# Decode attention over two caches on one core: who releases the value slot, when the denominators are gathered, and a projection on four column strips

## The chip, the cores and the metric

One core of one Trainium2 chip; the other cores are idle. The metric is the device time of one execution in microseconds (us), as the median of several executions. Ratios are computed as the mean time of one kernel's fast runs over that of the other's fast runs of the same rounds, so they are not quite the ratios of the medians quoted beside them. Where a sentence speaks of a "span", it is the profiled execution. In this kernel TensorE (PE in the profiles, PEld its weight loads) multiplies matrices into PSUM tiles, whose names begin with ps; DVE and ScalarE (ACT) copy and compute between PSUM and SBUF tiles; SP (its queue is SPq) issues the loads from device memory into SBUF.

## The reference, cut to what matters

Two attention blocks with one query token each, outputs concatenated. A has 32 heads with 32768 keys each; B has 32 query heads over 8 key heads, and only the last 4096 keys count.

```python
# A: q = x@wq; k, v: [32 heads, 32768 keys, 128]; out = softmax(q k^T / sqrt(128)) v, then @ wo
# B: the same with 8 key heads, each shared by 4 query heads, and a window of 4096 keys
o = einsum("bhqk,bhkd->bhqd", softmax(scores), v)
return concatenate([a, b], axis=-1)          # bf16, [1, 1, 1024]
```

So A alone reads 32 heads x (8 MiB of keys + 8 MiB of values), 537 MB of the 570 MB in all, and uses each byte once.

## The kernel before

Each head of A passes through these steps. SP issues all large loads in one queue, in the order K(0), V(0), K(1), V(1), ...; keys have three thirds of a buffer (a head uses two), values one slot of 8 MiB.

1. TensorE transposes the keys (8 per PSUM bank), DVE copies them to SBUF, TensorE makes scores on four column strips (psS).
2. DVE finds the maximum, ScalarE the exponentials (with the row sums in an extra column of `oc`), TensorE transposes them (psPT).
3. TensorE multiplies with the values, 64 matmuls on four strips, into psACC ("the products").
4. DVE sums four blocks of psACC into `oc` ("the sums"), and two small f32 matmuls gather `oc` into row g of psG: column 128 ("the denominators") and columns 0 to 127.

After the loop come the division, the spreading of A's and B's results to 128 partitions and the two projections with `wo`.

```python
    def emit_PV(self, name, g):
        ...                                  # 64 matmuls, c = 0..3 are column strips
        pv = self.op("pe", mm, self.landed("v", 0 if name == "A" else g), self.ptread, self.accread, to="dve")
        for i in (0, 1) if name == "A" else (g,):
            self.free["v"][i] = pv           # the next value load waits for this
        oc = t["oc"][g % 2][:, 0:DH]
        for j in range(4):                   # four sums on DVE, waiting for pv
            ...
        self.accread = o

    def emit_gather(self, name, g):
        ...
        for c, c2, to in ((DH, DH + 1, None), (0, DH, "dve")):
            self.gath = self.op("pe", lambda e, c=c, c2=c2: e.matmul(
                self.G[0:32, c0 + c:c0 + c2], lhsT=win, rhs=t["oc"][g % 2][:, c:c2], start=False, stop=True,
                skip_group_check=True), self.accread, self.sread, dep, to=to)
```

One thing in the helper matters. An operation raises one semaphore only, that of one waiting engine (`to`). If a second engine waits for it, the next operation of the same engine whose `to` is free carries that signal. Here the products signal DVE, and so the release of the value slot to SP is carried by the first gather matmul, which stands behind the four sums.

```python
    def emit_proj(self, name, bank, off):    # called for B, then for A
        for part in range(len(cuts) - 1):    # A's wo comes in 4 parts, B's in 2
            def mm(e, part=part):
                for a in range(cuts[part], cuts[part + 1]):     # 32 matmuls of 128x1 by 128x512
                    inst = e.matmul(bank[0:1, 0:512], lhsT=t["oz"][:, a:a + 1], rhs=wo[:, 512 * a:512 * a + 512],
                                    start=(a == 0), stop=(a == 31), skip_group_check=True)
            ...
```

## Time and profile before

| | |
|---|---|
| median of the first 3 runs | 1338.86 us (1338.84 to 1342.12) |
| median of 11 runs, three later sessions | 1342.8, 1342.33, 1341.78 us |
| span of the profiled run | 1340.9 us |
| last packet of the weights lands | 1332.25 us |

The page's head, its DMA row (busy tenths of the 16 DMA engines in 40 slices of the span) and the chain of waits by engine, kernel before:

```profile
span 1340.9 us, 28815 instructions
...
DMA  9999999999999999999999999999999999999996
...
DMA 68%; PE 28%; DVE 3%; issue 0%; ACT 0%; SPq 0%
```

Who the DMA queue's own sequencer (SPq) waited for; the first line is the value loads, the second mostly the key loads:

```profile
engine line waited for: us in total, times, longest us
SPq L283 <- PE psG L599: 743.7, 32, 23.9
SPq L283 <- PE psS L507: 524.9, 35, 27.8
```

And one head in the timeline (start, length, engine, line, what; in brackets the idle time before and what ended it):

```profile
894.27 6.10 PE L573 MATMUL psACC<-vbuf,ptsb 128*4 128x512 bf16 x64 [0.69 <-ACT ptsb L548]
...
900.43 0.35 DVE L585 TENSOR_SCALAR oc_A<-psACC,hot_A 128x128 f32<-128x128 f32 x1 [8.32 <-PE psACC L573]
900.81 1.12 DVE L587 SCALAR_TENSOR_TENSOR oc_A<-psACC,hot_A,oc_A 128x128 f32<-128x128 f32 x3
...
902.08 0.44 PE L599 MATMUL psG<-oc_A,hw 128*32 128x1 f32 x4 [1.72 <-DVE oc_A L587]
902.31 0.33 SPq L283 DMA_DIRECT2D vbuf<-in_A_v_cache_dram  x1
...
904.96 5.92 PE L485 MATMUL psT<-ident,kbuf 128*128 128x128 bf16 x64 [2.44 <-DMA kbuf<-in_A_k_cache_dram]
```

The products end at 900.37. The value load goes out 1.94 us later, at 902.31. The keys issued before it land at 904.92, so there were still 2.61 us of keys in flight. I call this distance the lead of the value issue.

The end of the kernel, the two projections and the last copy:

```profile
1323.32 8.36 PE L629 MATMUL psS<-kbuf,oz_B 128*1 128x512 bf16 x32
...
1331.52 7.07 PE L629 MATMUL psPT<-kbuf,oz_A 128*1 128x512 bf16 x32
...
1338.63 0.68 DVE L633 CAST out_sb<-psPT 1x512 bf16<-1x512 f32 x1 [6.23 <-PE psPT L629]
```

### The profile page before, as it was taken

To read this page: it belongs to the slowest core of one execution; us is meant where nothing else is said; L and a number is where in the kernel's file an instruction comes from. 1 tells how busy PE (TensorE), PEld (TensorE's weight loads), DVE (VectorE), ACT (ScalarE), POOL (GpSimd) and SP (SyncE) were. 2 spreads that over 40 slices of the span, in tenths; PEclk is the share of its full clock that TensorE was granted. 3 is DMA by queue.
4 is the path that set the end of the run, shared out by engine and by line. 5 is a ranking of instruction groups with operands and counts; after the bars stand their busy time and mean duration, and the time that the engine had idled before them with its cause. 6 is when DMAs were issued, how large, how long until landed. Compare 5 with 4: busy or idle time off the path is not lost.

```text
span 1340.9 us, 28815 instructions
## 1 busy us (share of the span) xinstructions
PE 960.0 (72%) x13272; PEld 667.2 (50%) x13272; DVE 804.6 (60%) x1660; ACT 54.8 (4%) x167; POOL 2.0 (0%) x15
## 2 busy tenths in 40 slices
PE   3756668776676877666786867678777667777777
PEld 3544446554444555444455544445555444555552
DVE  3655556765556676555676655566765555667572
ACT  0000000000000000000000000000000000000000
POOL 0000000000000000000000000000000000000000
PEclk9777788888778898787888878888887878888888
DMA  9999999999999999999999999999999999999996
GB/s 395 442 427 428 422 426 438 432 420 428 436 409 438 438 409 438 438 434 432 416 436 434 411 438 426 420 438 438 432 428 422 438 438 438 438 432 420 427 439 284
DMA packets 12932, 570.66 MB, mean 426 GB/s; under 512 B 1522, under 2 KB 1524, under 8 KB 1780
## 3 DMA queue, kind: packets, MB, share of 16 engines
q1 hardware_dynamic: 12628, 570.43, 99.0%
q8 instruction: 12, 0.20, 0.1%
q10 hardware_dynamic: 288, 0.00, 0.0%
q14 instruction: 4, 0.03, 0.0%
HBM read 570.43 MB, written 0.00 MB: 425 GB/s over the span
## 4 chain that ended last, share of the span: by engine, by line
DMA 68%; PE 28%; DVE 3%; issue 0%; ACT 0%; SPq 0%
DMA kbuf<-in_A_k_cache_dram 65%; PE psT L485 23%; PE psS L507 3%; DMA kbuf<-in_B_k_cache_dram 3%; DVE kt L488 3%; PE psACC L573 1%; PE psS L629 1%; PE psPT L629 1%; DVE oc_A L587 0%; ACT psb L535 0%; PE psPT L545 0%; DVE tr_in L524 0%; DVE b_A L530 0%; SPq L283 0%; DVE m L527 0%
## 5 line engine op out<-in xcount | busy, mean ns | idle before, releaser
L488 DVE COPY kt<-psT 128x1024 bf16<-128x1024 bf16 x1056 | 655.7, 684 | 210.2 <-PE psT L485 208.7
L485 PE MATMUL psT<-ident,kbuf 128*128 128x128 bf16 x8448 | 579.5, 234 | 137.5 <-DMA kbuf<-in_A_k_cache_dram 125.5
L485 PEld LDWEIGHTS psT<-ident,kbuf 128*128 128x128 bf16 x8448 | 540.1, 106 | 229.8 <-DMA kbuf<-in_A_k_cache_dram 133.6
L573 PE MATMUL psACC<-vbuf,ptsb 128*4 128x512 bf16 (+1 forms) x2112 | 189.2, 536 | 23.3 <-ACT ptsb L548 22.0
L507 PE MATMUL psS<-kt,qw 128*32 128x512 bf16 x2048 | 157.6, 385 | 15.5 <-DVE kt L488 15.5
L585 DVE TENSOR_SCALAR oc_A<-psACC,hot_A 128x128 f32<-128x128 f32 x32 | 11.2, 351 | 254.8 <-PE psACC L573 254.8
L573 PEld LDWEIGHTS psACC<-vbuf,ptsb 128*4 128x4 bf16 (+1 forms) x2112 | 61.0, 112 | 142.7 <-issue 95.6
L545 PE MATMUL psPT<-ident,psb 128*128 128x128 bf16 x136 | 20.2, 302 | 127.9 <-ACT psb L535 127.9
L545 PEld LDWEIGHTS psPT<-ident,psb 128*128 128x128 bf16 x136 | 11.5, 128 | 137.5 <-ACT psb L535 137.3
L535 ACT ACTIVATE psb<-psS,nb_A 128x512 bf16<-128x512 f32 x32 | 22.0, 687 | 1177.9 <-DVE nb_A L534 1177.9
L507 PEld LDWEIGHTS psS<-kt,qw 128*32 128x32 bf16 x2048 | 34.0, 95 | 58.0 <-DVE kt L488 31.4
L599 PE MATMUL psG<-oc_A,hw 128*32 128x128 f32 (+1 forms) x128 | 14.1, 220 | 54.9 <-DVE oc_A L587 54.9
L599 PEld LDWEIGHTS psG<-oc_A,hw 128*32 128x32 f32 x128 | 6.5, 109 | 70.1 <-issue 70.1
L587 DVE SCALAR_TENSOR_TENSOR oc_A<-psACC,hot_A,oc_A 128x128 f32<-128x128 f32 x96 | 33.7, 351 | 3.4
L524 DVE TENSOR_REDUCE tr_in<-psS 128x1 f32<-128x512 f32 x34 | 23.5, 692 | 17.5 <-PE psS L507 17.5
L527 DVE COPY m<-tr_a 1x16 f32<-1x16 f32 (+1 forms) x136 | 22.3, 164 | 2.6
L530 DVE COPY b_A<-mr_A 1x16 f32<-1x16 f32 x128 | 21.1, 165 | 2.4
L548 ACT ACTIVATE ptsb<-psPT 128x512 bf16<-128x512 bf16 x34 | 20.3, 597 | 30.5 <-PE psPT L545 30.5
L441 PE MATMUL psACC<-x_B,vbuf 128*128 128x1 bf16 x128 | 3.5, 165 | 13.2 <-DMA vbuf<-in_B_wq_dram 13.2
L441 PEld LDWEIGHTS psACC<-x_B,vbuf 128*128 128x128 bf16 x128 | 3.5, 104 | 13.1 <-issue 13.1
L629 PE MATMUL psS<-kbuf,oz_B 128*1 128x512 bf16 x32 | 8.4, 428 | 0.0
L525 DVE STREAM_TRANSPOSE tr_a<-tr_in 128x32 f32<-128x32 f32 x34 | 7.2, 212 | 1.2
(63 smaller groups left out, 83.8 us busy)
## 6 DMA issues: line engine op xcount, KB each, us to landing
kbuf<-in_B_k_cache_dram SPq DMA_DIRECT2D x2, 4096.0 KB, 32.5
vbuf<-in_B_v_cache_dram SPq DMA_DIRECT2D x2, 4096.0 KB, 23.9
kbuf<-in_A_k_cache_dram SPq DMA_DIRECT2D x2, 4096.0 KB, 23.9
vbuf<-in_B_wq_dram SPq DMA_DIRECT2D x1, 4096.0 KB, 12.3
vbuf<-in_A_wq_dram SPq DMA_DIRECT2D x1, 4096.0 KB, 32.4
kbuf<-in_B_wo_dram SPq DMA_DIRECT2D x2, 2048.0 KB, 31.2
kbuf<-in_A_wo_dram SPq DMA_DIRECT2D x1, 1536.0 KB, 28.7
kbuf<-in_A_wo_dram SPq DMA_DIRECT2D x1, 1280.0 KB, 31.5
```

The source lines that it names most:

```text
L485: inst = e.transpose(T[:, 128 * k:128 * k + 128], src[:, DH * k:DH * k + DH], self.ident[:, :])
L488: self.copies.append(self.op("dve", lambda v: v.tensor_copy(KT[:, :], T[:, :]), o, to="pe"))
L507: inst = e.matmul(self.S[32 * c:32 * c + 32, :], lhsT=win, rhs=self.kt[(bb + c // 2) % NKT][:, 512 * (c % 2):512 * (c % 2) + 512], start=b ...
L524: o = dve(lambda v: v.reduce_max(tr["in"][:, 0:1], self.S[:, :], axis=AXX), self.sdone, self.k_pool)
L527: x = dve(lambda v, c=c: v.tensor_copy(m4[0:1, W * c:W * c + W], tr["a"][32 * c:32 * c + 1, 0:W]), o)
L530: x = dve(lambda v, c=c: v.tensor_copy(t["b"][32 * c:32 * c + 1, 0:W].rearrange("p (k h) -> p k h", k=KC), t["mr"][0:1, :].unsqueeze(1).to ...
L535: self.sread = self.op("act", lambda s: s.activation(out=self.psb[:, :], in_=self.S[:, :], func=ACTF.Exp, bias=t["nb"][:, k:k + 1], scale= ...
L545: inst = e.transpose(PT[:, 128 * jj:128 * jj + 128], self.psb[:, 128 * jj:128 * jj + 128], self.ident[:, :])
L573: inst = e.matmul(acc[32 * c:32 * c + rows, 0:512], lhsT=lhsT, rhs=rhs, start=begin, stop=end, tile_position=(0, 32 * c), skip_group_check ...
L587: o = self.op("dve", lambda v, src=src, hot=hot: v.scalar_tensor_tensor(out=oc, in0=src, scalar=hot, in1=oc, op0=ALU.mult, op1=ALU.add), p ...
L599: self.gath = self.op("pe", lambda e, c=c, c2=c2: e.matmul(self.G[0:32, c0 + c:c0 + c2], lhsT=win, rhs=t["oc"][g % 2][:, c:c2], start=Fals ...
L629: inst = e.matmul(bank[0:1, 0:512], lhsT=t["oz"][:, a:a + 1], rhs=wo[:, 512 * a:512 * a + 512], start=(a == 0), stop=(a == 31), skip_group ...
```

## The change

Three intents: the next value load should go out as soon as the products have read the slot; the denominators (complete since the exponentials) should be gathered before the sums, and carry the signal to DVE that the products no longer can; and B's projection should use four column strips at once, its four partial rows being summed by one f32 matmul.

```diff
@@ build order @@
-            self.emit_gather("B", g)          # likewise for A; emit_PV now emits both gathers
-        self.emit_proj("B", self.S, 512)
-        self.emit_proj("A", self.PT, 0)
+        self.emit_proj()
@@ emit_PV @@
-        pv = self.op("pe", mm, ..., self.accread, to="dve")
+        pv = self.op("pe", mm, ..., self.accread, to="sp")
         for i in (0, 1) if name == "A" else (g,):
             self.free["v"][i] = pv
+
+        pv = self.emit_gather(name, g, DH, DH + 1)      # denominators; the sums wait for this
         ...
         self.accread = o
+        self.gath = self.emit_gather(name, g, 0, DH)
@@ projections (cut) @@
+    def emit_proj(self):
+        for part in range(len(self.WO_CUTS["B"]) - 1):
+            o = self.proj_part("B", part, lambda a: (self.S[32 * (a % 4):32 * (a % 4) + 1, :], (0, 32 * (a % 4)), a < 4, a >= 28))
+        strips = self.op("dve", lambda v: v.tensor_copy(self.pb[:, :], self.S[:, :]), o)
+        for part in range(len(self.WO_CUTS["A"]) - 1):
+            last = self.proj_part("A", part, lambda a: (self.PT[0:1, :], None, a == 0, a == 31))
+            if part == 0:
+                o = self.op("pe", lambda e: e.matmul(self.ACC[0:1, :], lhsT=self.e32[:, 0:1], rhs=self.pb[:, :],
+                                                     start=True, stop=True, skip_group_check=True), strips, self.accread)
+                self.store("B", self.ACC, 512, o)
+        self.store("A", self.PT, 0, last)
```

More of the change, by code (lines that the diff above doesn't have):

```diff
@@ L243, in alloc @@
         self.m4 = sb("m4", [1, 128], F32)
+        self.pb = sb("pb", [128, 512], F32)
         self.out_sb = sb("out_sb", [1, 1024], BF16)
@@ L385, in plan @@
             self.emit_PV("A", g)
-            self.emit_gather("A", g)
         self.loop = {}
@@ L575, in mm @@
             return inst
-        pv = self.op("pe", mm, self.landed("v", 0 if name == "A" else g), self.ptread, self.accread, to="dve")
+        pv = self.op("pe", mm, self.landed("v", 0 if name == "A" else g), self.ptread, self.accread, to="sp")
         for i in (0, 1) if name == "A" else (g,):
             self.free["v"][i] = pv
+        pv = self.emit_gather(name, g, DH, DH + 1)
         oc = t["oc"][g % 2][:, 0:DH]
@@ L589, in emit_PV, with emit_gather @@
         self.accread = o
+        self.gath = self.emit_gather(name, g, 0, DH)
     GCOL = {"A": 0, "B": 256}
-    def emit_gather(self, name, g):
+    def emit_gather(self, name, g, c, c2):
         t, HG, c0 = self.c[name], self.X[name]["HG"], self.GCOL[name]
         win = self.hw[:, :] if name == "A" else t["hsel"][:, 32 - HG * g:64 - HG * g]
-        dep = self.hcopy if name == "A" else self.k_sel
-        for c, c2, to in ((DH, DH + 1, None), (0, DH, "dve")):
-            self.gath = self.op("pe", lambda e, c=c, c2=c2: e.matmul(
-                self.G[0:32, c0 + c:c0 + c2], lhsT=win, rhs=t["oc"][g % 2][:, c:c2], start=False, stop=True,
-                skip_group_check=True), self.accread, self.sread, dep, to=to)
+        return self.op("pe", lambda e: e.matmul(
+            self.G[0:32, c0 + c:c0 + c2], lhsT=win, rhs=t["oc"][g % 2][:, c:c2], start=False, stop=True,
+            skip_group_check=True), self.accread, self.sread, self.hcopy if name == "A" else self.k_sel, to="dve")
     def emit_spread(self, name):
@@ L618, in emit_spread, with proj_part, mm @@
         t["ozop"] = self.op("dve", lambda v: v.tensor_copy(t["oz"][:, :], p2[:, 0:32]), o)
-    def emit_proj(self, name, bank, off):
-        t = self.c[name]
-        cuts = self.WO_CUTS[name]
-        off_wo = HALF * DH * self.wo_third(name)
-        wo = self.kbuf[:, off_wo:off_wo + HALF * DH]
-        for part in range(len(cuts) - 1):
-            def mm(e, part=part):
-                inst = None
-                for a in range(cuts[part], cuts[part + 1]):
-                    inst = e.matmul(bank[0:1, 0:512], lhsT=t["oz"][:, a:a + 1], rhs=wo[:, 512 * a:512 * a + 512],
-                                    start=(a == 0), stop=(a == 31), skip_group_check=True)
-                return inst
-            o = self.op("pe", mm, (self.wosem[name][part], 16), t["ozop"])
-        o = self.op("dve", lambda v: v.tensor_copy(self.out_sb[0:1, off:off + 512], bank[0:1, 0:512]), o)
+    def proj_part(self, name, part, out):
+        a0, a1 = self.WO_CUTS[name][part:part + 2]
+        oz, wo = self.c[name]["oz"], self.kbuf[:, HALF * DH * self.wo_third(name):]
+        def mm(e):
+            inst = None
+            for a in range(a0, a1):
+                row, pos, begin, end = out(a)
+                inst = e.matmul(row, lhsT=oz[:, a:a + 1], rhs=wo[:, 512 * a:512 * a + 512], start=begin, stop=end,
+                                tile_position=pos, skip_group_check=True)
+            return inst
+        return self.op("pe", mm, (self.wosem[name][part], 16), self.c[name]["ozop"])
@@ L634, in emit_proj, with store @@
+    def store(self, name, bank, off, dep):
+        o = self.op("dve", lambda v: v.tensor_copy(self.out_sb[0:1, off:off + 512], bank[0:1, :]), dep)
         self.op("sp", lambda e: e.dma_start(self.out[0, :, off:off + 512], self.out_sb[0:1, off:off + 512])
                 .then_inc(self.outsem[name], 16), o)
+    def emit_proj(self):
[9 more added lines that the diff above has]
+        self.store("A", self.PT, 0, last)
```

## The prediction

> **What bounds the kernel now.** The profile's slice table shows the DMA engines at nine tenths or more in every slice but the last. By the packet list a 64 KB packet takes about 2.42 us, so sixteen engines move one head's 16.8 MB of keys and values in about 38.7 us; the key issues of the queue's timeline are 39.03 us apart on average (133.85 to 1226.67 us, 28 heads). This agrees with the Trainium skill, "DMA: Bandwidth & Descriptors", section Specifications (435 GB/s fabric ceiling): most slices move 420 to 438 GB/s. The chain of waits is 68% DMA. Summed over the packets, the engines are idle only about 2.6 us between 40 and 1320 us. TensorE is 72% busy and waits for keys at each head.
>
> **The value slot.** Today the value load waits, by the queue's waits, for the gather matmul (743.7 us over 32 loads). In the timeline it is issued about 1.9 us after the products end (1288.57 against about 1286.6), since four DVE sums of 0.35 us and a matmul stand between. After the change it goes out about 1.9 us earlier. But it is already issued 3 to 5 us before the keys ahead of it in the same queue have landed (626.43 against 631.1; 666.91 against 670.2). The queue isn't dry, so this mainly lengthens the queue. It can recover at most the 2.6 us of idle engine time, and only where the engine that lands last was the idle one: I expect 0.7 us.
>
> **The denominators.** No work is removed. The 128x1 gather (two instructions) moves from behind the sums to before them; the sums now wait for it. Per head about 0.2 us moves from one side to the other; net zero within 0.1 us, and hidden by the key load in all but the last two heads.
>
> **The end.** This is where the gain is. From 1323.3 us on TensorE alone is critical: B's projection, 32 matmuls, 8.3 us (0.43 us each while the granted clock was half, until 1326.1, then 0.21), A's 7.0 us, then copy and store: 2.3 us to the end. The last packet of A's weights lands at 1332.25, so A's parts hardly wait. With four strips B's matmuls should overlap in fours, as the value products in the same geometry do: 64 of them take 5.5 to 6.0 us, 0.43 us per four at half clock, about 0.22 at full. Eight groups, mostly at half clock: about 3.1 us, saving 5.2. The extra f32 matmul that sums the strips stands in TensorE's order behind A's first part; estimated at 0.9 us (two passes at up to twice the bf16 time of 0.21). The 128x512 copy (about 0.7 us) hides behind A's 12 first matmuls, and B's store behind the rest of A. Net -4.3 us. The weights' landing gives a floor only about 1 us below that.
>
> **Predicted time:** 1338.9 - 4.3 - 0.7, about 1334 us (-0.4%). Range 1331.0 to 1337.3. Chances: faster by over 2% 0.01, within 2% 0.98, slower 0.01.
>
> **What would show it.** Queue waits name the products instead of the gather; value issues come about 1.9 us earlier, with issue to landing longer by as much (23.7 to about 25.5 us) and key landings 39.0 us apart as before. B's 32 projection matmuls span about 3 us, A's about 8 with the strip sum inside; the wait before A's last four is under 1 us.
>
> **What would make it wrong.** Strips that do not overlap at one output row (gain near zero); an f32 matmul of 2 us or more; the last weights landing later, so that A's last part waits; or the engines' idle time lying wholly on the one that lands last (2 us more). Runs of before differ by 3 us, which is nearly the gain.

## More of the kernel before

One line of the view of a stretch, from the issue of A's first key load to that of head 30 (the thirty-first), has at its end the share of time that the 16 engines were busy and the rate that they moved:

```profile
core 0: us, PE busy (x) PEld busy (x) DVE busy (x) ACT busy (x) POOL busy (x), PEclk, DMA share, GB/s
55.80:1226.70 1170.90, 842.12 (x11612) 587.20 (x11604) 714.59 (x1462) 47.45 (x149) 0.00 (x0) 0.83 1.00 430
```

DMA share 1.00 at 430 GB/s.

## The result, and the profile after

The changed kernel took 1331.92 us (median of 4 runs, 1331.31 to 1332.46), against 1340.49 us (4 runs) before: ratio 0.9935, interval 0.9915 to 0.9955. Two later repeats with more rounds gave 1331.66 against 1342.33 us (0.9924, 0.9907 to 0.9941) and 1331.71 against 1341.78 us (0.9921, 0.9905 to 0.9936). So the gain is 8.6 to 10.7 us, and the spread between runs shrinks: 2.4 us or less within each session, against 4 to 8 us before (4 runs of each in the first session, where it was 1.2 against 4.0 us; later 6 against 11).

The page after, and the same stretch (first to thirty-first key issue):

```profile
span 1330.5 us, 28787 instructions
...
DMA  9999999999999999999999999999999999999997
```

```profile
core 0: us, PE busy (x) PEld busy (x) DVE busy (x) ACT busy (x) POOL busy (x), PEclk, DMA share, GB/s
56.40:1220.30 1163.90, 838.30 (x11612) 589.07 (x11604) 713.80 (x1462) 47.50 (x149) 0.00 (x0) 0.84 1.00 433
```

The DMA share is 1.00 as before, but the engines moved 433 GB/s instead of 430, and the thirty heads took 1163.9 us instead of 1170.9. In this pair of profiles that is the larger part of the gain, and it is invisible in the busy share.

The queue's waits now name the products, as intended:

```profile
SPq L284 <- PE psACC L571: 683.5, 32, 22.1
SPq L284 <- PE psS L505: 579.0, 35, 28.2
```

A head of the changed kernel, at about the same time. It is value load 22, the one after the load shown above, and its lead is below the changed kernel's median of 5.66 us:

```profile
926.17 5.93 PE L571 MATMUL psACC<-vbuf,ptsb 128*4 128x512 bf16 x64 [0.69 <-ACT ptsb L546]
...
931.93 0.20 PE L598 MATMUL psG<-oc_A,hw 128*32 128x1 f32 x2
932.15 0.33 SPq L284 DMA_DIRECT2D vbuf<-in_A_v_cache_dram  x1
932.20 0.35 DVE L585 TENSOR_SCALAR oc_A<-psACC,hot_A 128x128 f32<-128x128 f32 x1 [8.20 <-PE psG L598]
932.59 1.12 DVE L587 SCALAR_TENSOR_TENSOR oc_A<-psACC,hot_A,oc_A 128x128 f32<-128x128 f32 x3
...
933.77 0.41 PE L598 MATMUL psG<-oc_A,hw 128*32 128x128 f32 x2 [1.64 <-DVE oc_A L587]
...
937.12 5.37 PE L483 MATMUL psT<-ident,kbuf 128*128 128x128 bf16 x64 [2.94 <-DMA kbuf<-in_A_k_cache_dram]
```

The value load goes out 0.05 us after the products' modelled end (932.10), and 4.92 us before the keys land (937.07). The sums wait for the denominators' gather and start 0.10 us after the products.

The end:

```profile
1317.15 3.29 PE L627 MATMUL psS<-kbuf,oz_B 128*1 128x512 bf16 x32
...
1320.27 2.75 PE L627 MATMUL psPT<-kbuf,oz_A 128*1 128x512 bf16 x12
...
1322.86 1.02 PE L645 MATMUL psACC<-pb,e 128*1 128x512 f32 x2
...
1323.71 4.48 PE L627 MATMUL psPT<-kbuf,oz_A 128*1 128x512 bf16 x20
...
1328.23 0.68 DVE L633 CAST out_sb<-psPT 1x512 bf16<-1x512 f32 x1 [3.64 <-PE psPT L627]
```

B's 32 matmuls took 3.29 us instead of 8.36, the f32 matmul put 0.85 us between A's parts (1322.86 to 1323.71), and nothing waits for weights. From the landing of head 30's keys to the end of the span it was 83.0 us instead of 86.8: 3.8 us gained here. The other 6.6 us of the two spans' difference of 10.4 came before, from the loop.

### Where the loop's time was hidden

The trace has a record for each DMA packet. A load of 8 MiB is 128 packets of 64 KB on 16 DMA engines, with 16 closing packets of 4 bytes; so each engine has 8 large packets of a load, one after the other, and one closing packet. I call one engine's sequence of packets a ring. The records carry no ring number: where rings are told apart, the closing packet of the keys is paired, in order of time, with the value packet that starts after it. A 64 KB packet of a key or value row takes 2.42 us at the median of both kernels, but the means between 56 and 1227 us differ: 2.436 us before, 2.425 us after. I counted, from the records, by how much the packets exceed 2.418 us (summed, divided by 16 engines, "stretch"), and how long engines had no packet at all ("idle"):

```
                                    before      after
stretch in the loop                 8.64 us     3.33 us
  of it within 4 us of a value issue  6.59 us   1.69 us
packets over 2.8 us                  128          29
idle in the loop                     2.56 us     0.54 us
lead of the value issue, median      3.85 us     5.66 us
  smallest to largest                2.6 to 5.7  4.3 to 8.0
```

Stretch and idle fell by 7.3 us together, against 6.9 us of shorter loop. That these two agree is bookkeeping, since the same packets were moved; it is the place that tells something. Of the 5.3 us that the stretch fell, 4.9 us lay within 4 us of a value issue; away from them it went only from 2.05 to 1.64 us. Of the 128 long packets before, 121 started within 4 us after a value issue (21 of 29 after). The long packets in the head shown are each ring's first of the value load. In the head at 902.31 above, 15 of the 16 rings ran out of keys between 903.1 and 903.6 us, about 1 us after the value issue; their first value packets took 2.9 to 3.4 us. The last ring ran out at 904.6 us, and its first value packet took 2.42 us. The landing of the keys, which the timeline shows, is that of the slowest ring: it says nothing of the other 15.

### The profile page after: what moved, and what is told of

It is laid out like the page before. It is cut to its first block, busy times and chain, and to the rows that moved or that the text cites. A ratio compares the mean times of both kernels' runs of the same rounds, so it can differ in the third digit from the quotient of the medians.

```text
span 1330.5 us, 28787 instructions
## 1 busy us (share of the span) xinstructions
PE 953.2 (72%) x13274; PEld 668.9 (50%) x13274; DVE 805.0 (61%) x1661; ACT 54.8 (4%) x167; POOL 2.0 (0%) x15
## 4 chain that ended last, share of the span: by engine, by line
DMA 68%; PE 28%; DVE 3%; issue 0%; ACT 0%; SPq 0%
DMA kbuf<-in_A_k_cache_dram 65%; PE psT L483 23%; PE psS L505 3%; DMA kbuf<-in_B_k_cache_dram 3%; DVE kt L486 3%; PE psACC L571 1%; PE psPT L627 1%; PE psS L627 0%; DVE oc_A L587 0%; ACT psb L533 0%; PE psPT L543 0%; DVE tr_in L522 0%; DVE b_A L528 0%; DVE m L525 0%; SPq L284 0%
## 5 line engine op out<-in xcount | busy, mean ns | idle before, releaser
L585 DVE TENSOR_SCALAR oc_A<-psACC,hot_A 128x128 f32<-128x128 f32 x32 | 11.2, 351 | 255.5 <-PE psG L598 255.5
L598 PE MATMUL psG<-oc_A,hw 128*32 128x128 f32 (+1 forms) x128 | 19.3, 227 | 52.3 <-DVE oc_A L587 52.3
L598 PEld LDWEIGHTS psG<-oc_A,hw 128*32 128x32 f32 x128 | 11.4, 109 | 62.4 <-DVE oc_A L587 55.0
## 6 DMA issues: line engine op xcount, KB each, us to landing
vbuf<-in_B_v_cache_dram SPq DMA_DIRECT2D x2, 4096.0 KB, 23.7
vbuf<-in_B_wq_dram SPq DMA_DIRECT2D x1, 4096.0 KB, 12.3
```

Of the source, the lines that this page charges most:

```text
L598: return self.op("pe", lambda e: e.matmul(self.G[0:32, c0 + c:c0 + c2], lhsT=win, rhs=t["oc"][g % 2][:, c:c2], start=False, stop=True, ski ...
```

## The experiments

Theory 1: a value load that is issued while most rings are about to run out stalls each of them, and the stall hides inside packets that count as busy; releasing the slot earlier removes it. Theory 2 (the prediction's): the loop cannot gain more than its idle time, and the gain is in the end. Theory 3: the loop gained by the new order of gather and sums, not by the release.

The loop in the table goes from the first to the thirty-first key issue in the one profiled run. Three profiles of the changed kernel gave 1164.0, 1161.7 and 1166.1 us, so a difference of 3 us in this column alone means little. The kernel before was profiled once. Taken together, the three profiles with the old moment of release (before, strips_only, late_release) have loops of 1167.3 to 1170.8 us, mean 1168.6, and the six with early release and whole value loads 1161.7 to 1166.1 us, mean 1163.7: about 5 us, less than the 6.9 us of the first pair. In the rows split_slot and both_tails the long packets and the stretch are those of the keys' 64 KB packets alone; the values come in 32 KB packets there.

| run | median us | before, same session | ratio (95%) | loop us | median lead us | packets over 2.8 us | stretch + idle us |
|---|---|---|---|---|---|---|---|
| before | | | | 1170.8 | 3.85 | 128 | 11.2 |
| after | 1331.92 | 1340.49 | 0.9935 (0.9915-0.9955) | 1164.0 | 5.66 | 29 | 3.9 |
| strips_only | 1337.87 | 1342.8 | 0.9968 (0.9946-0.9989) | 1167.8 | 3.81 | 95 | 8.7 |
| release_only | 1336.56 | 1342.8 | 0.9951 (0.993-0.9972) | 1163.5 | 5.89 | 27 | 3.0 |
| late_release | 1337.08 | 1342.8 | 0.9961 (0.9941-0.9982) | 1167.3 | 3.99 | 86 | 7.9 |
| later_release | 1355.09 | 1342.8 | 1.0095 (1.0073-1.0116) | 1177.8 | 2.38 | 209 | 18.9 |
| after_again | 1331.66 | 1342.33 | 0.9924 (0.9907-0.9941) | 1161.7 | 5.49 | 19 | 2.9 |
| sums_first | 1332.45 | 1342.33 | 0.993 (0.9913-0.9947) | 1163.3 | 5.90 | 20 | 3.1 |
| split_slot | 1333.14 | 1342.33 | 0.9933 (0.9916-0.995) | 1166.1 | 7.77 | 4 | 1.1 |
| both_tails | 1332.42 | 1342.33 | 0.9929 (0.9913-0.9946) | 1166.1 | 7.80 | 3 | 1.0 |
| after_third | 1331.71 | 1341.78 | 0.9921 (0.9905-0.9936) | 1166.1 | 5.46 | 49 | 5.3 |
| a_strips | 1331.56 | 1341.78 | 0.9917 (0.9902-0.9932) | 1163.6 | 5.41 | 39 | 3.9 |

All outputs are right.

### strips_only: the new projection alone

```diff
 # the kernel before, with only
+        self.emit_proj()                     # and proj_part, store, pb of the changed kernel
-        self.emit_proj("B", self.S, 512)
-        self.emit_proj("A", self.PT, 0)
```

> The kernel before with only the new last projection (four strips for B, one f32 matmul that sums them); the value slot is released late, as before. Theory 1 (late value loads let some DMA rings run dry, and the stall is hidden inside packets that count as busy): the loop stays as before, 1170.8 us from the first to the thirty-first key issue, value issues 2.6 to 5.3 us ahead of the key landing; only the end shortens, landing of the last-but-one keys to end of span from 86.8 to about 83 us: -3.8 us, ratio about 0.997. Theory 2 (the loop is unchanged within noise, all of the gain is in the end): the full -8.6 us, ratio 0.9935. B's 32 matmuls span about 3.3 us under both.

It gained 0.32%, 4.3 us by the ratio. The lead stayed as before (3.81 us). The loop was 3 us shorter and there were 95 long packets instead of 128; the expected 1170.8 us was missed by what one profile can't resolve. From head 30's keys to the end it was 83.8 us instead of 86.8. B's matmuls spanned 3.27 us. So the end is worth 3 to 4.5 us, about what the prediction said, and not the whole gain: theory 2 falls.

### release_only: the new release with the old projection

```diff
 # the changed kernel, with
-        self.emit_proj()
+        self.emit_proj("B", self.S, 512)
+        self.emit_proj("A", self.PT, 0)
```

> The changed kernel with the old last projection: value slot released by the products, denominators ahead of the sums. Theory 1: loop 1164 us from the first to the thirty-first key issue instead of 1170.8, value issues 4.3 to 6.8 us ahead of the key landing, few packets of value or key loads over 2.5 us just after a value issue; end as before, 86.8 us; -5 us in total, ratio about 0.996. Theory 2: within 1 us of before, ratio 1.000.

```profile
core 0: us, PE busy (x) PEld busy (x) DVE busy (x) ACT busy (x) POOL busy (x), PEclk, DMA share, GB/s
55.70:1219.20 1163.50, 838.73 (x11612) 589.03 (x11604) 713.75 (x1462) 47.49 (x149) 0.00 (x0) 0.84 1.00 433
```

It gained 0.49%, 6.6 us by the ratio (3.8 to 9.4 by its interval); the line above is the loop stretch of this run, 433 GB/s as in the changed kernel. Its end was as long as before (87.6 us). The prediction had given this part 0.7 us. The two parts alone add up to 0.81%; together they gave 0.65 to 0.79%.

### late_release: the new order, but the old moment of release

```diff
 # the changed kernel, with
-        pv = self.op("pe", mm, ..., to="sp")            # and free["v"] = pv
+        pv = self.op("pe", mm, ...)
...
-        self.gath = self.emit_gather(name, g, 0, DH)
+        late = self.emit_gather(name, g, 0, DH // 2, to="sp")
+        self.free["v"][i] = late                        # for both halves
+        self.gath = self.emit_gather(name, g, DH // 2, DH)
```

(The gather of the sums is cut in two, since one operation carries one signal; with a single gather to SP, the division on DVE waits for a signal that never comes.)

> The changed kernel (denominators ahead, strips) but with the value slot released by the first half of the gather of the sums, about 2 us after the products, as before. Theory 1: loop back to about 1170.8 us, only the end's gain is left: ratio about 0.997, as strips_only. Theory 3 (the new order of gather and sums, not the release, makes the loop shorter): the loop stays at 1164 us, ratio 0.9935.

```profile
SPq L284 <- PE psG L599: 743.8, 32, 23.9
```

```profile
core 0: us, PE busy (x) PEld busy (x) DVE busy (x) ACT busy (x) POOL busy (x), PEclk, DMA share, GB/s
54.70:1222.00 1167.30, 835.95 (x11674) 589.94 (x11666) 712.76 (x1462) 47.51 (x149) 0.00 (x0) 0.84 1.00 431
```

The queue waits for the gather again, and of the whole change's gain only that of the end is left: 0.39%, with 86 long packets. Its median, 1337.08 us, is that of strips_only (1337.87, same session), not of the changed kernel (1331.7). The changed kernel did not run beside it; but the lowest of late_release's six runs, 1335.8 us, is above the highest of the changed kernel's sixteen in three sessions, 1333.11, while the medians of the kernel before differ by 2.3 us between sessions. The extra matmul of the split gather costs nothing at the end, which took 83.1 us. Theory 3 falls: the order of gather and sums does not shorten the loop, the moment of release does.

### later_release: the cost made larger

```diff
 # the kernel before, with, after the gather of each head of A
+            for k in range(2):
+                late = self.op("dve", lambda v, k=k: v.memset(self.scr[k][:, :], 0.0), to="sp" if k else None)
+            self.free["v"] = [late, late]
```

> The kernel before with the value slot released later still: two writes of scratch on DVE stand between the sums and the release, in all about 1 to 2 us more. The keys' own landing is not touched by these, as TensorE waits over 2.6 us for them there. Theory 1: lead of the value issue over the key landing falls to about 1 to 3.5 us, and the stall grows at least in proportion: loop longer by 10 to 40 us (0.3 to 1.3 us a head), long packets in every head. Theory 2: the loop doesn't change (under 2 us), since the value load is still queued before the keys have landed; only the last two heads add some 1 to 4 us at the end.

```profile
904.91 0.33 SPq L284 DMA_DIRECT2D vbuf<-in_A_v_cache_dram  x1
...
908.37 6.10 PE L489 MATMUL psT<-ident,kbuf 128*128 128x128 bf16 x64 [5.04 <-DMA kbuf<-in_A_k_cache_dram]
```

```profile
core 0: us, PE busy (x) PEld busy (x) DVE busy (x) ACT busy (x) POOL busy (x), PEclk, DMA share, GB/s
56.00:1233.80 1177.80, 836.27 (x11612) 581.75 (x11604) 766.85 (x1520) 47.49 (x149) 0.00 (x0) 0.84 1.00 427
```

The two writes (0.91 us each) cut the median lead to 2.38 us, and the kernel became 12.3 us slower in the medians. In the profiles 6.9 us of it are the loop and 2.4 us the end, where the writes stand in the chain of the last two heads. Each value issue still came before its keys had landed, yet the rate fell to 427 GB/s at a DMA share of 1.00. So theory 2's reasoning ("the queue isn't dry") fails directly. The loop's loss was smaller than the 10 to 40 us that I expected: leads alternate, 16 of 30 were between 1.3 and 2.6 us and paid 0.4 to 0.8 us of stretch each, with the idle time 0.8 to 1.8 us, while the other 14 were over 3 us and paid next to nothing. Long packets in every head, as expected, there were not.

The packet records of four profiles (before, after, strips_only, later_release; 30 heads x 16 rings each) show how the loss depends on what a ring still has to do. The 7 rings of 1920 whose keys had run out before the issue are left out. For each other ring, I took how long after the value issue its keys ran out, the gap to its first value packet, and that packet's duration:

```
keys of the ring run out        rings   gap     first value packet   lost per ring
  0   to 0.5 us after issue       72    0.69 us       3.15 us           1.42 us
  0.5 to 1                       255    0.39          3.12              1.09
  1   to 1.5                     123    0.21          2.93              0.72
  1.5 to 2                       149    0.06          2.60              0.24
  2   to 2.5                     180    0.04          2.50              0.12
  2.5 to 3                       489    0.01          2.47              0.06
  3   to 4                       384    0.01          2.43              0.02
  over 4                         261    0.01          2.42              0.01
```

Of the rings that ran out within 1 us, the first value packet ended 4.2 us after the issue (median). With 2.42 us per packet, I estimate from this that a ring needs 1.8 us of queued work at the next issue; in the table the loss falls to 0.24 us at 1.5 to 2 us and to 0.12 us or less beyond. Every ring that runs out earlier loses, whatever the slowest one does.

### after_again and sums_first: do the sums lose by waiting for the gather?

> The changed kernel itself, run again as the yardstick for the three beside it. Theory 1: ratio to before 0.993 to 0.995, loop (first to thirty-first key issue) 1163.5 to 1164.5 us, landing of the last-but-one keys to the end 83.0 us. Theory 2 and 3 say the same, this run doesn't separate them.

The ratio came as expected, 0.9924. The loop, 1161.7 us, and the end, 84.1 us, both lay outside: one profile does not fix them to 1 us.

```diff
 # the changed kernel, with
-        pv = self.op("pe", mm, ..., to="sp")
+        pv = self.op("pe", mm, ..., to="dve")           # the sums wait for the products
-        pv = self.emit_gather(name, g, DH, DH + 1)
+        self.emit_gather(name, g, DH, DH + 1, to="sp")  # carries the release
```

> The changed kernel, but the sums wait for the products themselves, and the denominators' gather, which stands between products and sums on TensorE, releases the value slot. If putting the gather in front of the sums costs time on the critical path, it costs it only in the last two heads: sums start 0.05 us after the products instead of 0.3 us, so the end shortens by 0.3 to 0.5 us (83.0 to about 82.6), the value issue comes about 0.2 us later, and the loop stays within 1 us of the changed kernel's. Total within 1 us of it.

1332.45 against 1331.66 us: no gain from letting the sums start directly. The expected 0.3 to 0.5 us is below what these runs resolve; the 83.5 us of its end lies within the 82.4 to 84.1 us of the changed kernel's three profiles. Swapping the two signals is neutral, as predicted for the denominators.

### split_slot: still more lead, at a price

```diff
 # sums_first, with
-        self.load(self.vbuf[:, :], self.kv_src("v", "A", g)[:, 0, :], self.mark("v", 0), *self.free["v"])
+        for i in range(2):                              # two loads of 4 MiB
+            self.load(self.vbuf[:, w * i:w * i + w], src[:, w * i:w * i + w], self.mark("v", i), self.free["v"][i])
...
+            self.free["v"][0] = self.op("pe", lambda e: mm(e, todo[:32]), self.landed("v", 0), ..., to="sp")
+            pv = self.free["v"][1] = self.op("pe", lambda e: mm(e, todo[32:]), self.landed("v", 1), to="dve")
```

> As sums_first, with each value load cut in two halves of 4 MB; the first half of the products (in key order) releases the first half of the slot, about 3 us before the products end. Theory 1: the lead of the value issue over the key landing grows to 7 us or more, the long packets just after a value issue disappear (under 0.3 us summed, 1.7 us in the changed kernel), and the loop falls to its packet floor, 30 heads of 16 packets of 2.418 us, 1160.6 us, so 1161 to 1162.5 us: 2 to 3 us less than the changed kernel. Rival: the remaining distance from the floor has nothing to do with the lead (or smaller packets of 32 KB move slower), then the loop stays at 1164 us or grows.

The lead grew to 7.77 us, and the long packets are gone: 4 are left, stretch near a value issue 0.26 us, no idle time. (The value packets are now of 32 KB, so that even a stretched one would stay under 2.8 us; but of 7620 only 4 took over 1.4 us.) Yet the kernel was no faster, 1333.14 us. The rival in my expectation fits: a 32 KB packet took 1.218 us at the median, so two take 2.436 us instead of 2.42. For 8 pairs per ring and 30 heads that is 3.8 us ((2.436 - 2.420) x 8 x 30), more than the 1 to 3 us of stalls near value issues that were left to save in the changed kernel's three profiles. My figure of 1161 to 1162.5 us for the loop was wrong by that.

### both_tails and a_strips: A's projection on strips too

```diff
 # split_slot (both_tails) or the changed kernel (a_strips), with
+        # A's parts 0 to 2 on four strips of psT2, DVE copies them to pa;
+        # part 3 unstripped into psT1, then one f32 matmul adds the strips there
```

> As split_slot, with A's first three parts of the projection on four strips too; A's last part, which lands last, is added unstripped in the same bank as the matmul that sums A's strips. End from landing of the last-but-one keys: about 80.5 us instead of 83, loop as split_slot; total 4 to 5.5 us below the changed kernel, about 1326.5 to 1328 us, ratio to before about 0.990. Were the end bound by the last weights' landing rather than TensorE, it would gain under 1 us.

> The changed kernel a third time, as the yardstick for a_strips on the same chip: 1331 to 1332.5 us, ratio to before 0.992 to 0.9945.

> The changed kernel with A's first three parts of the projection on four strips too, value loads whole (64 KB packets). In both_tails TensorE waited for A's weights at the end because its loop was slower by 32 KB packets; here the weights should land about 2 us earlier. End from landing of the last-but-one keys about 81 us instead of 83 to 84; total 1.5 to 2.5 us below the changed kernel on the same chip, about 1329.5 to 1330.5 us. If the landing of the last weights already sets the end of the changed kernel, nothing is gained.

Both missed. both_tails took 1332.42 us instead of 1326.5 to 1328, 0.7 us less than split_slot. a_strips took 1331.56 us, the changed kernel 1331.71 us in the same session. The end of a_strips shows why:

```profile
1324.43 0.59 PE L628 MATMUL psT<-kbuf,oz_A 128*1 128x512 bf16 x6 [1.28 <-DMA kbuf<-in_A_wo_dram]
...
1325.66 1.02 PE L628 MATMUL psT<-kbuf,oz_A 128*1 128x512 bf16 x4 [0.64 <-DMA kbuf<-in_A_wo_dram]
```

TensorE now waits for A's third and fourth parts of the weights. It did so in both_tails too, and the whole value loads, which a_strips' expectation counted on, did not remove these waits. From the landing of the last weights to the end of the span the kernel before had 8.65 us, the changed kernel 5.0 to 6.6 us in its three profiles, and a_strips 4.7 us. So a_strips' end is set by the landing of the weights and the work that has to follow it: four matmuls, the f32 matmul, the copy and the store. No version measured here clearly beats the changed kernel.

## Why the prediction was right or wrong

**The time.** 1334 us was predicted, 1331.92 measured, inside the range of 1331.0 to 1337.3. That is partly luck: the starting point of 1338.9 us was the median of three runs, and larger samples put the kernel before at 1341.8 to 1342.8 us. The predicted difference was 5 us, the measured one 8.6 to 10.7 us: the starting point was too low and the gain too small, and the two errors partly cancel.

**The end: right.** "Net -4.3 us" against 3.8 us between the two profiles and 4.3 us in strips_only. B's matmuls were predicted at 3.1 us and took 3.29; the f32 matmul at 0.9 us and took 0.85 between its neighbours. A's projection with the sum inside spans 7.9 us, predicted about 8. The floor set by the weights, "about 1 us below", fits a_strips, which took work off TensorE there and came out only 0.15 us lower.

**The release: mechanism seen, size wrong.** The queue waits, the 1.9 us earlier issue (median lead 3.85 to 5.66 us) and the longer time from issue to landing (23.7 to 25.1 us, predicted 25.5) came as said. The failed step is this: "It can recover at most the 2.6 us of idle engine time ... I expect 0.7 us." release_only measured 6.6 us. Two inferences failed. First, that idle time is the upper bound: 6.6 us of stretch stood next to the value issues inside packets that count as busy. The prediction itself held the contradiction: 38.7 us of packets per head against key issues 39.03 us apart are 0.33 us per head, some 10 us in thirty heads, of which 2.6 us of idle time explain only a quarter. Second, "the queue isn't dry" was judged by the landing of the keys, hence by the slowest ring; in the median head before, the first ring ran out 2.4 us after the value issue, in 12 of 30 heads within 1.8 us (4 of 30 after). "Key landings 39.0 us apart as before" was wrong by the same step: from the first to the thirty-first key issue 1170.8 / 30 = 39.03 us before, 1164.0 / 30 = 38.80 us after (the landings give the same), where 16 packets of 2.418 us take 38.69 us.

**The denominators: right.** Neutral within what can be resolved (sums_first), and not the loop's cause (late_release).

**Open.** What a ring does inside a stretched packet is not shown; the records give only its start and its duration. Nor is it shown why the kernel before varies more between runs; its leads lie where the loss in the table above begins, which would fit, but no run tests it. That the moment of release is the cause rests on runs that moved it; that a single ring's loss is set by its own remaining work is read from the records, not tested.

## What to carry to other kernels

When a kernel is DMA-bound, compare the rate with what the usual packet duration would give, and look at the tail of packet durations; a busy share of 1.00 does not exclude stalls (here it stood beside 433, 430 and 427 GB/s). Issue each load while the fastest ring, not the slowest, still has work, here about 2 us with 64 KB packets; the slot's release hung behind four sums and a matmul only because one signal per operation was already taken. Splitting the value load to gain lead was paid for here in slower small packets (0.7% per byte), so first move the signal.

## What the Trainium skill lacked or had wrong

- "Perfetto Trace Analysis", section DMA Engine Tracks, says that a DMA engine's slices show actual busy time, idle time excluded. Here packets of the same 64 KB took 2.42 us in a full queue and 3.13 us on average when their ring had under 1 us of work left at the issue; the rate was 433 GB/s in the changed kernel and 427 in later_release, with a DMA share of 1.00 in both. So a slice's length is not the time that its bytes need.
- "DMA: Bandwidth & Descriptors", section Specifications, gives a first-byte latency of about 0.6 us for loads issued from SP. In four profiles a value load's first packet on a ring nearly always started 0.95 us or later after the start of the issue, which itself takes 0.33 us; counted from its end that is 0.62 us, close to the page's figure. But the first value packet took near its usual 2.42 us (2.50 us and less on average) only on rings with 2 us or more of work left. The page has no figure for how early the next load must be queued.
- The same section's fabric ceiling of 435 GB/s agrees: 433 GB/s were reached in the loop (slices of the page of the kernel before go up to 442, but each packet is counted whole in the slice in which it starts). The page's "Rules for kernel authors" ask for at least 1 MiB per DMA; beyond that, in loads of 4 and 8 MiB, 32 KB rows still cost 0.7% more per byte than 64 KB rows (2 x 1.218 against 2.42 us), a figure that no page has.
- "TensorE: Matmul & The Clock Gate", Part 3, lists 2.38 times for three column strips. With four strips and one output row each, a group of four matmuls took 0.43 us, the same as one unstripped matmul at the same half clock, so four times here; both from the spacing of B's weight loads in the two timelines.
